# Attention and a gated feed-forward in one kernel: GpSimd's long instructions cut into pieces of 128 columns, and a pair of small VectorE instructions moved

## The chip, the cores and the metric

One Trainium2 chip; the kernel runs on one of its cores. The metric is the device time of a run in microseconds (us), lower is better. Engines: TensorE (PE, its weight loads PEld), VectorE (DVE), ScalarE (ACT), GpSimd (POOL), SyncE (SP), which issues most of the loads and stores.

## The reference

Attention over 4 batches, 8 heads, 576 tokens and 64 dimensions a head, with rotary positions on q and k, then a feed-forward of width 1024 with a convolution of three taps along the tokens and a gate:

```
q_rot, k_rot = rotate(q), rotate(k)      # [x1*cos - x2*sin, x1*sin + x2*cos]
scores = scale * q_rot @ k_rot^T
attn = exp(scores - max) / (sum + 1e-9)
x = (attn @ v) as [4, 576, 512]
h = max(x @ w_in, 0)
conv_out = conv_w[0]*h[s-1] + conv_w[1]*h[s] + conv_w[2]*h[s+1]
out = (h * sigmoid(conv_out)) @ w_out
```

The three weights reach the kernel as 64-bit floats; it converts them to 32 bits itself. q, k and v are 32-bit floats.

## The kernel before

The unit of attention is a pair of heads, p = 0 to 15. For each, q and k (512 of the tokens as [128, 4 x 2 x 64], "rq" and "rk"; the other 64 of both together, "rr") are loaded, rotated by `rope`, transposed on PE (`emit_TQ`), multiplied to scores (`emit_S`), reduced and turned into exponentials (`soft`: `negm` on DVE at L214, `st` on ACT at L218), transposed again (`emit_T`, `emit_Trem`), and multiplied with v (`emit_E`). For p=0 DVE does the rope of q and r, and POOL that of k; for all others POOL does all three. A rope is four instructions: two products with the tables of cosines and sines (L143 and L149, 512 columns for q or k, 128 for r), and two sums of half the columns (L155 and L156).

The sums of the exponentials come out of ACT's accumulator as `sums`, one column for each block of 128 queries. `emit_rinv` adds 1e-9 and takes the reciprocals on DVE, 9 columns each (L289, L290). `emit_rinvT` transposes these on PE (L295), copies them out ("rst"), and sends them through DRAM to come back spread over the partitions ("rb"), by which `norm` multiplies the product with v on DVE (L328).

The weights come in 16 pieces of 128 x 512. Each is converted by one ACT and four DVE instructions (`to_f32`: L446 to L460), then split into a high part, rounded by ACT (L503), and a low part, the difference, by POOL (L504). `conv_w` goes through the same code with 32 x 128 elements ("cwf"). The products of the feed-forward (`emit_M1` at L347, `emit_M2` at L425) use high and low parts. Between them DVE does the convolution (L359, L361) and the gate (L370), ACT the hyperbolic tangent, and ACT and POOL split the results ("g", at L378 and L379), as they split the attention's result ("xT", L332 and L333).

The order of the instructions is written out by hand: each engine runs its own in the order of emission. A plan holds entries (step, rank, function); five steps belong to a pair of heads. Within a step the ranks set the order, those of 10 and more come last, and after some entries a counter moves on, by which deferred work (`defer`) is emitted. Up to step 26 (`WIDE`) attention runs with the conversion of the weights; from there with the feed-forward's products, which are woven between the entries of rank 2 and 4; the last two blocks of the feed-forward run alone. The transposes of q, r and k of pair p stand at the steps 5p-4, 5p-3 and 5p-2 (`emit_TQ`), its ropes at 5p-8 and 5p-6. In the first stage ACT does the copies of `emit_Trem`, later DVE (L164). The instructions are placed like this:

```
at(max(n - 8, 0), 18, lambda p=p: rope(p, "q", nc.gpsimd))
at(max(n - 6, 0), 18, lambda p=p: rope(p, "k", nc.gpsimd))
at(n + 5, 4, lambda p=p: emit_E(p, 1))
at(n + 5, 1.7, lambda p=p: emit_rinv(p))
at(n + 6, 2, lambda p=p: emit_rinvT(p))
```

Of the kernel before, what the change touches and what calls it, by code (L numbers as in the profile page):

```python
# [7 lines left out]
F32 = mybir.dt.float32  # L8
# [4 lines left out]
ALU = mybir.AluOpType  # L13
# [7 lines left out]
def attention_moe_kernel(ctx, tc, q, k, v, w_in, conv_w, w_out, tab, out):  # L21
    nc = tc.nc
# [53 lines left out]
    def defer(k, fn, rank=1):  # L76
        due.setdefault(slot[0] + k, []).append((rank, len(due.get(slot[0] + k, [])), fn))
# [58 lines left out]
    def rope(p, part, eng):  # L136
        x = raw[p][part]
        n = 2 if part == "r" else 8
        if part != "r":
            x = x.rearrange("p t h d -> p (t h) d")  # L140
        c, s = (cosr, sinr) if part == "r" else (cosm, sinm)
        t1 = rot[p, part] = p1.tile([128, n, D], F32, tag="t1" + part, name="t1")
        eng.tensor_tensor(  # L143
            out=t1.rearrange("p n (e i) -> p n e i", e=2),
            in0=x.rearrange("p n (e i) -> p n e i", e=2),
            in1=c.unsqueeze(2).to_broadcast([128, n, 2, 32]),
            op=ALU.mult,
        )
        eng.tensor_tensor(  # L149
            out=x.rearrange("p n (e i) -> p n e i", e=2),  # L150
            in0=x.rearrange("p n (e i) -> p n e i", e=2),
            in1=s.unsqueeze(2).to_broadcast([128, n, 2, 32]),
            op=ALU.mult,
        )
        eng.tensor_tensor(out=t1[:, :, 0:32], in0=t1[:, :, 0:32], in1=x[:, :, 32:64], op=ALU.subtract)  # L155
        eng.tensor_tensor(out=t1[:, :, 32:64], in0=t1[:, :, 32:64], in1=x[:, :, 0:32], op=ALU.add)  # L156

    QT, KT = {}, {}

# [35 lines left out]
    def go(d, key):  # L195
        for fn in d.pop(key):
            fn()
# [58 lines left out]
    def emit_T(p, s, h=None):  # L256
        if p not in PT:
            PT[p] = ptp.tile([128, 9, S], F32, tag="pt", name="pt")
        pt = PT[p]
        ps = t_tile()  # L260
        st = STR[p] if s == 4 else ST[p, s][:, h, 64 * h:64 * h + 512]
        for t in range(4):
            nc.tensor.transpose(ps[:, 128 * t:128 * t + 128], st[:, 128 * t:128 * t + 128], idf)  # L263
        if s == 4:
            evac("A", pt[:, 0:8, 512:S], ps.rearrange("p (k c) -> p k c", k=8))
        else:
            evac("A", pt[:, h:8:2, 128 * s:128 * s + 128], ps.rearrange("p (k c) -> p k c", k=4))

    def emit_Trem(p, g):
        pt = PT[p]  # L270
        ps = t_tile()
        if g < 2:
            for u in range(2):
                x = ST[p, 2 * g + u].rearrange("p h k -> p (h k)")[:, 512:640]
                nc.tensor.transpose(ps[:, 128 * u:128 * u + 128], x, idf)
            evac("V", pt[:, 8, 256 * g:256 * g + 256], ps[:, 0:256])
        else:
            for h in range(2):
                x = strem[p % 2][:, 512 - 64 * h:640 - 64 * h]
                nc.tensor.transpose(ps[:, 128 * h:128 * h + 128], x, idf)  # L280
            for h in range(2):
                r = slice(64 * h, 64 * h + 64)
                evac("V", pt[r, 8, 512:S], ps[r, 192 * h:192 * h + 64])
# [3 lines left out]
    def emit_rinv(p):  # L287
        s = p % 2
        nc.vector.tensor_scalar(out=sums[p], in0=sums[p], scalar1=1e-9, scalar2=None, op0=ALU.add)  # L289
        nc.vector.reciprocal(out=rvc[s][:, 0:9], in_=sums[p])  # L290

    def emit_rinvT(p):
        s = p % 2
        ps = t_tile()[0:32, 0:128]
        nc.tensor.transpose(ps, rvc[s], idf)  # L295
        st = p1.tile([32, 128], F32, tag="rst", name="rst")
        evac("V", st, ps)
        d = scr.tile([9, 128], F32, tag="d", name="rd")
        nc.sync.dma_start(out=d, in_=st[0:9, :])
        fl = d.rearrange("(o t) n -> o (t n)", o=1)  # L300
        rbt = rb[p] = p1.tile([128, S], F32, tag="rb", name="rb")
        nc.sync.dma_start(out=rbt[0:64, :], in_=fl[:, 0:S].to_broadcast([64, S]))
        nc.sync.dma_start(out=rbt[64:128, 0:512], in_=fl[:, 640:1152].to_broadcast([64, 512]))
        nc.sync.dma_start(out=rbt[64:128, 512:S], in_=fl[:, 576:640].to_broadcast([64, 64]))
# [132 lines left out]
    def to_f32(pool, w64, w, n):  # L437
        w32 = w64.bitcast(I32).rearrange("p (n t) -> p n t", t=2)
        h, l = w32[:, :, 1], w32[:, :, 0]
        t = pool.tile([128, n], I32, tag="wt", name="wt")[0:w64.shape[0]]  # L440

        def first():
            nc.scalar.activation(out=t.bitcast(F32), in_=h.bitcast(F32), func=AF.Abs)  # L443

        def clamp():
            nc.vector.tensor_scalar(  # L446
                out=t.bitcast(F32), in0=t.bitcast(F32), scalar1=bits(F32_TINY), scalar2=bits(F32_HUGE),
                op0=ALU.max, op1=ALU.min,
            )

        def second():
            nc.vector.tensor_scalar(
                out=t, in0=t, scalar1=3, scalar2=0x3FFFFFFF, op0=ALU.logical_shift_left, op1=ALU.bitwise_and
            )
            nc.vector.scalar_tensor_tensor(
                out=t, in0=l, scalar=29, in1=t, op0=ALU.logical_shift_right, op1=ALU.bitwise_or
            )

        def third():
            nc.vector.scalar_tensor_tensor(  # L460
                out=w.bitcast(I32), in0=h, scalar=-(1 << 30), in1=t, op0=ALU.bitwise_and, op1=ALU.bitwise_or
            )

        return first, clamp, second, third
# [11 lines left out]
    def load_w(i):  # L476
        if i >= len(WPIECES):
            return
        src, _, _, kk, c = WPIECES[i]
        t = late["ws"].tile([128, 512], I64, tag="w64", name="w64", bufs=3)  # L480
        nc.sync.dma_start(out=t, in_=src[kk * 128:kk * 128 + 128, c:c + 512])
        stage[i] = t

    def conv_w_piece(i):
        _, dh, dl, kk, c = WPIECES[i]
        box = {}

        def first():
            box["w"] = late["ws"].tile([128, 512], F32, tag="wf", name="wf")
            box["s"] = to_f32(late["ws"], stage.pop(i), box["w"], 512)  # L490
            box["s"][0]()

        def mid():
            box["s"][1]()
            box["s"][2]()

        def third():
            box["s"][3]()
            load_w(i + 3)
            hi, lo = dh[:, kk, c:c + 512], dl[:, kk, c:c + 512]  # L500

            def split():
                nc.scalar.activation(out=hi, in_=box["w"], func=AF.Copy)  # L503
                nc.gpsimd.tensor_tensor(out=lo, in0=box["w"], in1=hi.bitcast(F32), op=ALU.subtract)  # L504

            defer(2, split)

        return [first, mid, third]
# [36 lines left out]
    def at(n, rank, fn):  # L545
        plan.setdefault(n, []).append((rank, len(plan.get(n, [])), fn))

    def emit():
        with tc.manual_schedule(engines=engines):
            load(0)  # L550
            for x in rvc + krem + [x[:, S:S + 64] for x in strem]:
                nc.vector.memset(x, 0.0)
            rope(0, "q", nc.vector)
            rope(0, "k", nc.gpsimd)
            rope(0, "r", nc.vector)
            for part in "qrk":
# [8 lines left out]
            for p in range(1, NP):  # L565
                n = STEPS * p
# [8 lines left out]
            for p in range(NP):  # L575
                n = STEPS * p
                for s in range(STEPS):
                    m = n + s
                    first = m < WIDE
                    if m:  # L580
                        at(m - 1 if first else m, 0.5 if first else 0, lambda p=p, s=s: emit_S(p, s))
                    at(m, 0.2, lambda p=p, s=s: go(reds, (p, s)))
                    at(m, 0.3 if first else 1.5, lambda p=p, s=s: go(exps, (p, s)))
                    for h in range(2 if s < 4 else 1):
                        at(m + 1, 0 if m + 1 < WIDE else 1, lambda p=p, s=s, h=h: emit_T(p, s, h))
                for g, e in ((0, 2), (1, 4), (2, 5)):
                    at(n + e, 2, lambda p=p, g=g: emit_Trem(p, g))
                at(n + 4, 4, lambda p=p: emit_E(p, 0))
                at(n + 5, 4, lambda p=p: emit_E(p, 1))
                at(n + 5, 1.7, lambda p=p: emit_rinv(p))  # L590
                at(n + 6, 2, lambda p=p: emit_rinvT(p))
                for j in range(2):
                    at(n + 8, 1.7 + j, lambda p=p, j=j: norms.pop((p, j))())
            nw = len(wsteps)
            for i, u in enumerate(wsteps):
                x = (WIDE - 1) * i // nw
# [114 lines left out]
```

## Time and profile before

| | |
|---|---|
| time, median of 3 runs | 556.59 us (555.76 to 556.72) |
| span of the profiled execution, first to last instruction | 553.1 us |
| PE busy | 508.9 us (92%) |
| DVE busy | 386.5 us (70%) |
| ACT busy | 325.1 us (59%) |
| POOL busy | 273.2 us (49%), 341 instructions |

The profile is of one execution, and its own time is known as its span; the median of the runs is 3.5 us above that. A busy share is an average over stages that differ. Matmuls are pipelined, and a busy PE may still wait between two of them. An instruction's duration includes the time in which it has started and can't go on.

### The profile page before, as it was taken

The page shows a single profiled execution, that of the slowest core. Times are in us where ns is not written, and L with a number is a line of the kernel's source. Part 1 is how long each engine was busy: PE and PEld are TensorE (multiplying, and loading weights), DVE is VectorE, ACT ScalarE, POOL GpSimd, SP SyncE. Part 2 cuts the span into 40 slices and gives each one's busy share as a digit, 9 for nine tenths or more (in the row PEclk, how much of TensorE's full clock was granted, in tenths as well). Part 3 has the DMA queues.
Part 4 walks back from the last instruction along what each step waited for, and adds up shares of the span by engine and source line. Part 5 has one row for each costly group of instructions (what it writes and reads, how often), then busy time and mean ns, then how long its engine had stood idle before and what let it go on. Part 6 is the DMA issues. An engine that isn't in the chain of part 4 may idle for free.

```text
span 553.1 us, 9298 instructions
## 1 busy us (share of the span) xinstructions
PE 508.9 (92%) x3295; PEld 369.3 (67%) x3295; DVE 386.5 (70%) x624; ACT 325.1 (59%) x870; POOL 273.2 (49%) x341
## 2 busy tenths in 40 slices
PE   2797969788999899999999999999999999999997
PEld 1354444445767477776877677777768677879986
DVE  4878977896588837684768747692677646657961
ACT  2779766877758545675747546663557546324530
POOL 4666857587573817383555637291361203232440
PEclk9999989999999999999999999999999999999999
DMA  7434433423303031030302140210300110000011
GB/s 187 130 101 130 121 104 97 142 75 71 87 1 87 1 83 24 24 84 7 99 2 66 40 106 1 62 45 26 101 0 24 41 42 0 29 33 20 2 38 58
DMA packets 67538, 33.08 MB, mean 60 GB/s; under 512 B 60412, under 2 KB 61220, under 8 KB 67492
## 3 DMA queue, kind: packets, MB, share of 16 engines
q1 hardware_dynamic: 66292, 32.10, 21.0%
q8 instruction: 26, 0.43, 0.3%
q10 hardware_dynamic: 1200, 0.39, 0.3%
q14 instruction: 20, 0.16, 0.1%
HBM read 27.68 MB, written 4.79 MB: 59 GB/s over the span
## 4 chain that ended last, share of the span: by engine, by line
PE 65%; DVE 15%; ACT 14%; issue 3%; DMA 2%; SPq 0%; ACTq 0%; DVEq 0%
PE tp L316 12%; PE sp L206 11%; PE pm L425 10%; PE pm L347 9%; PE tp L263 9%; PE mt L425 6%; ACT st L218 6%; PE mt L347 5%; DVE c L361 5%; ACT pt L162 4%; DVE negm L214 3%; DVE c L359 2%; PE tp L185 1%; DVE xn L328 1%; ACT wt L443 1%
## 5 line engine op out<-in xcount | busy, mean ns | idle before, releaser
L162 ACT ACTIVATE pt<-tp 128x512 f32<-128x512 f32 (+2 forms) x164 | 88.0, 562 | 93.1 <-PE tp L263 91.5
L214 DVE TENSOR_REDUCE negm<-sp 128x1 f32<-128x576 f32 x144 | 102.4, 748 | 39.5 <-PE sp L206 39.2
L379 POOL TENSOR_TENSOR g<-c,g 128x288 fp32r<-128x288 f32 (+4 forms) x88 | 57.0, 659 | 142.9 <-ACT g L378 141.3
L206 PE MATMUL sp<-kT,qT 64*128 64x288 f32 (+4 forms) x556 | 103.9, 470 | 1.2 <-ACT st L218 0.9
L218 ACT ACTIVATE st<-sp,negm 128x576 f32<-128x576 f32 x128 | 93.8, 746 | 15.1 <-DVE negm L214 15.1
L361 DVE SCALAR_TENSOR_TENSOR c<-rr,cw,c 128x288 f32<-128x288 f32 x128 | 96.7, 755 | 4.5
L263 PE MATMUL tp<-tabs,st 128*128 128x128 f32 x512 | 73.9, 285 | 20.3 <-ACT kr L162 7.6
L263 PEld LDWEIGHTS tp<-tabs,st 128*128 128x128 f32 x512 | 56.0, 143 | 46.2 <-issue 14.5
L347 PE MATMUL pm<-xT,winh 128*128 128x290 f32 x384 | 82.8, 308 | 0.5 <-ACT rr L355 0.5
L316 PE MATMUL tp<-pt,vm 128*64 128x290 f32 x512 | 69.6, 414 | 3.7 <-ACT pt L162 3.4
L206 PEld LDWEIGHTS sp<-kT,qT 64*128 64x128 f32 (+1 forms) x556 | 46.6, 177 | 36.0 <-issue 16.7
L425 PE MATMUL pm<-wouth,g 128*128 128x512 f32 x176 | 63.1, 412 | 0.0
L347 PEld LDWEIGHTS pm<-xT,winh 128*128 128x128 f32 x384 | 61.2, 190 | 1.4 <-ACT rr L355 0.7
L347 PE MATMUL pm<-xT,winl 128*128 128x290 f32 x192 | 56.9, 296 | 0.0
L370 DVE SCALAR_TENSOR_TENSOR c<-c,rr 128x288 f32<-128x288 f32 x64 | 39.1, 610 | 20.9 <-ACT c L367 20.2
L316 PEld LDWEIGHTS tp<-pt,vm 128*64 128x64 f32 x512 | 34.0, 136 | 28.8 <-ACT pt L162 5.1
L143 POOL TENSOR_TENSOR t<-rq,tabs 128x512 f32<-128x512 f32 x15 | 20.0, 1334 | 62.7 <-DMA rq<-q 62.1
L367 ACT ACTIVATE c<-c 128x288 f32<-128x288 f32 x64 | 28.3, 443 | 20.8 <-DVE c L361 20.5
L359 DVE TENSOR_SCALAR c<-rr,cw 128x288 f32<-128x288 f32 x64 | 31.2, 488 | 12.0 <-ACT rr L355 11.3
L425 PEld LDWEIGHTS pm<-wouth,g 128*128 128x128 f32 x176 | 33.1, 188 | 9.3 <-issue 2.2
L324 ACT ACTIVATE xn<-tp 128x290 f32<-128x290 f32 x32 | 13.2, 414 | 42.5 <-PE tp L316 42.5
L333 POOL TENSOR_TENSOR xT<-xn,xT 128x290 fp32r<-128x290 f32 x32 | 28.4, 892 | 18.2 <-ACT xT L332 16.9
(97 smaller groups left out, 883.6 us busy)
## 6 DMA issues: line engine op xcount, KB each, us to landing
out<-ot SPq DMA_DIRECT2D x17, 256.0 KB, 2.4
rk<-k SPq DMA_DIRECT2D x32, 128.0 KB, 3.0
w<-moe_w_in SPq DMA_DIRECT2D x8, 512.0 KB
vm<-v SPq DMA_DIRECT2D x32, 128.0 KB, 2.4
w<-moe_w_out SPq DMA_DIRECT2D x8, 512.0 KB, 3.4
rq<-q SPq DMA_DIRECT2D x30, 128.0 KB, 2.5
rb<-rd SPq DMA_DIRECT2D x16, 144.0 KB, 2.9
rb<-rd SPq DMA_DIRECT2D x16, 128.0 KB, 3.0
```

The costliest lines, as they stand in the source:

```text
L162: nc.scalar.activation(out=out, in_=in_, func=AF.Copy, scale=1.0 if sc is None else sc)
L206: nc.tensor.matmul(out=out, lhsT=qt[64 * h:64 * h + 64, c], rhs=kt[64 * h:64 * h + 64, a:a + n], start=True, stop=True)
L214: reds.setdefault((p, s), []).append(lambda: nc.vector.tensor_reduce(out=nm, in_=sc, axis=AX.XY if len(sc.shape) == 3 else AX.X, op=ALU.ma ...
L218: lambda: nc.scalar.activation(out=dst, in_=sc, func=AF.Exp, bias=nm, scale=1.0, accum_out=sm)
L263: nc.tensor.transpose(ps[:, 128 * t:128 * t + 128], st[:, 128 * t:128 * t + 128], idf)
L316: nc.tensor.matmul(out=xp[64 * h:64 * h + 64, 0:XW], lhsT=vmain[p][:, h, i, :] if i < 4 else vrem[p % 2][:, h, :], rhs=PT[p][:, 2 * i + h ...
L347: nc.tensor.matmul(out=ps[:, 0:XW], lhsT=w[:, kk, fs], rhs=xT[:, xs, e, :], start=(i == 0), stop=(i == n - 1))
L359: nc.vector.tensor_scalar(out=c, in0=r[:, j:j + HS], scalar1=cw[:, f:f + 1], scalar2=None, op0=ALU.mult)
L361: nc.vector.scalar_tensor_tensor(out=c, in0=r[:, j + e:j + e + HS], scalar=cw[:, 8 * e + f:8 * e + f + 1], in1=c, op0=ALU.mult, op1=ALU.add,)
L370: nc.vector.scalar_tensor_tensor(out=c, in0=c, scalar=1.0, in1=r[:, j + 1:j + 1 + HS], op0=ALU.add, op1=ALU.mult)
L379: nc.gpsimd.tensor_tensor(out=lo, in0=c[:, o:o + n], in1=hi.bitcast(F32), op=ALU.subtract)
L425: nc.tensor.matmul(out=ops[tt][:, 0:width], lhsT=g_tile(tt, f, e), rhs=w[:, f, cols], start=(f == 0 and i == 0), stop=(f == NF - 1 and i = ...
```

## The change

Two edits. In `rope`, where POOL does it, the two products go over two of the eight head blocks at a time (128 columns), and the two sums over four (128 columns of output); DVE's ropes stay whole. The low part of a piece of the weights is computed in four instructions of 128 columns. And `emit_rinv` moves from rank 1.7 to rank 4.5 of its step, behind the product with v of rank 4.

```diff
-        eng.tensor_tensor(
-            out=t1.rearrange("p n (e i) -> p n e i", e=2),
-            in0=x.rearrange("p n (e i) -> p n e i", e=2),
-            in1=c.unsqueeze(2).to_broadcast([128, n, 2, 32]),
-            op=ALU.mult,
-        )
...
-        eng.tensor_tensor(out=t1[:, :, 0:32], in0=t1[:, :, 0:32], in1=x[:, :, 32:64], op=ALU.subtract)
-        eng.tensor_tensor(out=t1[:, :, 32:64], in0=t1[:, :, 32:64], in1=x[:, :, 0:32], op=ALU.add)
+        t2, x2 = t1.rearrange("p n (e i) -> p n e i", e=2), x.rearrange("p n (e i) -> p n e i", e=2)
+        m = n if eng is nc.vector else 2
+        for dst, tb in ((t2, c), (x2, s)):
+            for a in range(0, n, m):
+                w = slice(a, a + m)
+                eng.tensor_tensor(
+                    out=dst[:, w], in0=x2[:, w], in1=tb[:, w].unsqueeze(2).to_broadcast([128, m, 2, 32]), op=ALU.mult
+                )
+        m = n if eng is nc.vector else min(n, 4)
+        for a in range(0, n, m):
+            w = slice(a, a + m)
+            eng.tensor_tensor(out=t1[:, w, 0:32], in0=t1[:, w, 0:32], in1=x[:, w, 32:64], op=ALU.subtract)
+            eng.tensor_tensor(out=t1[:, w, 32:64], in0=t1[:, w, 32:64], in1=x[:, w, 0:32], op=ALU.add)
...
-                nc.gpsimd.tensor_tensor(out=lo, in0=box["w"], in1=hi.bitcast(F32), op=ALU.subtract)
+                for o in range(0, 512, 128):
+                    w = slice(o, o + 128)
+                    nc.gpsimd.tensor_tensor(out=lo[:, w], in0=box["w"][:, w], in1=hi[:, w].bitcast(F32), op=ALU.subtract)
...
-                at(n + 5, 1.7, lambda p=p: emit_rinv(p))
+                at(n + 5, 4.5, lambda p=p: emit_rinv(p))
```

On POOL, at the start of the program, the rope of k of p=0 and the first instructions of that of q of p=1 stand like this before:

```order
L143 TENSOR_TENSOR t_118<-rk,tabs 128x512
L149 TENSOR_TENSOR rk<-rk,tabs 128x512
L155 TENSOR_TENSOR t_118<-t_118,rk 128x8x32
L156 TENSOR_TENSOR t_118<-t_118,rk 128x8x32
L512 MEMSET cw_177 32x256
L143 TENSOR_TENSOR t_195<-rq,tabs 128x512
```

And now, in the same place (the lines of the changed kernel have other numbers):

```order
L148 TENSOR_TENSOR t_118<-rk,tabs 128x128 x4
L148 TENSOR_TENSOR rk<-rk,tabs 128x128 x4
L154 TENSOR_TENSOR t_118<-t_118,rk 128x4x32
L155 TENSOR_TENSOR t_118<-t_118,rk 128x4x32
L154 TENSOR_TENSOR t_118<-t_118,rk 128x4x32
L155 TENSOR_TENSOR t_118<-t_118,rk 128x4x32
L514 MEMSET cw_185 32x256
L148 TENSOR_TENSOR t_203<-rq,tabs 128x128 x4
```

A rope of four instructions is now twelve; nothing else moved on POOL, and the order of its work is the same.

On DVE, in the step of the sums and reciprocals of p=5, the first pair of heads whose pair of instructions moved in the order, the queue is this before:

```order
L214 TENSOR_REDUCE negm<-sp 128x1 x2
L289 TENSOR_SCALAR sums<-sums 128x9
L290 RECIPROCAL rvc_83<-sums 128x9
L164 COPY pt<-tp 64x64 x2
L370 SCALAR_TENSOR_TENSOR c<-c,rr_1423 128x288
L359 TENSOR_SCALAR c<-rr_1424,cw 128x288
L361 SCALAR_TENSOR_TENSOR c<-rr_1424,cw,c 128x288 x2
L214 TENSOR_REDUCE negm<-sp 128x1 x2
```

And now:

```order
L213 TENSOR_REDUCE negm<-sp 128x1 x2
L163 COPY pt<-tp 64x64 x2
L369 SCALAR_TENSOR_TENSOR c<-c,rr_1575 128x288
L358 TENSOR_SCALAR c<-rr_1576,cw 128x288
L360 SCALAR_TENSOR_TENSOR c<-rr_1576,cw,c 128x288 x2
L288 TENSOR_SCALAR sums<-sums 128x9
L289 RECIPROCAL rvc_83<-sums 128x9
L213 TENSOR_REDUCE negm<-sp 128x1 x2
```

The pair went behind the copies, the gate of one part of the feed-forward and the convolution of the next. For p=5, 7, 9, 11, 13 and 15 it is so; for p=6, 8, 10, 12 and 14 the pair goes behind the two copies alone; for p=0 to 4 its place among DVE's instructions is the same. The queues of PE, ACT and SP are the same in both kernels.

## Rows read from the trace of the kernel before

**Rows 1.** The page's chain of waits that ended last, by engine.

```profile
PE 65%; DVE 15%; ACT 14%; issue 3%; DMA 2%; SPq 0%; ACTq 0%; DVEq 0%
```

**Rows 2.** Busy by stage: stretch, PE, PEld, DVE, ACT, POOL, granted clock, DMA share, GB/s.

```profile
14.00:146.00 132.00, 109.45 (x672) 62.14 (x669) 106.50 (x140) 100.50 (x260) 89.35 (x103) 0.96 0.37 104
146.00:411.00 265.00, 259.56 (x1758) 192.77 (x1757) 185.16 (x302) 159.36 (x433) 141.40 (x176) 1.00 0.19 48
```

**Rows 3.** Single lines on DVE: duration in ns, min/median/max, first and last start.

```profile
L361 DVE SCALAR_TENSOR_TENSOR c<-rr,cw,c x128: 517/522/1601, 147.7 to 531.5; 128x288 f32<-128x288 f32 x128
...
L214 DVE TENSOR_REDUCE negm<-sp x144: 694/748/760, 15.3 to 462.4; 128x1 f32<-128x576 f32 x144
...
L446 DVE TENSOR_SCALAR wt<-wt x17: 403/433/1387, 19.0 to 125.6; 128x512 f32<-128x512 f32 x16, 32x128 f32<-32x128 f32 x1
```

**Rows 4.** The same for lines of the rope on POOL.

```profile
L143 POOL TENSOR_TENSOR t<-rk,tabs x16: 1262/1366/1573, 6.6 to 405.5; 128x512 f32<-128x512 f32 x16
...
L143 POOL TENSOR_TENSOR t<-rr,tabs x15: 448/456/669, 15.7 to 403.7; 128x128 f32<-128x128 f32 x15
...
L155 POOL TENSOR_TENSOR t<-t,rk x16: 722/732/1054, 9.4 to 408.6; 128x256 f32<-128x256 f32 x16
```

**Rows 5.** Timeline of the start: start us, duration us, instruction.

```profile
6.64 1.26 POOL L143 TENSOR_TENSOR t<-rk,tabs 128x512 f32<-128x512 f32 x1 [6.20 <-DMA rk<-k]
6.67 1.51 DVE L156 TENSOR_TENSOR t<-t,rq 128x256 f32<-128x256 f32 x1
...
10.06 0.76 POOL L156 TENSOR_TENSOR t<-t,rk 128x256 f32<-128x256 f32 x1
...
11.37 1.06 PE L185 MATMUL tp<-tabs,t 128*128 128x128 f32 x4
```

**Rows 6.** Timeline: the end of the rope of q, p=1, and its transposes.

```profile
14.98 0.72 POOL L156 TENSOR_TENSOR t<-t,rq 128x256 f32<-128x256 f32 x1
...
20.29 0.66 PE L185 MATMUL tp<-tabs,t 128*128 128x128 f32 x4
```

**Rows 7.** Timeline of two places in the first stage; in brackets, idle time and releaser.

```profile
18.96 1.22 DVE L446 TENSOR_SCALAR wt<-wt 128x512 f32<-128x512 f32 x1
...
73.98 1.19 DVE L446 TENSOR_SCALAR wt<-wt 32x128 f32<-32x128 f32 x1 [3.48 <-ACT wt L443]
...
75.77 1.27 DVE L460 SCALAR_TENSOR_TENSOR cwf<-cw,wt 32x128 int32<-32x128 int32 x1
...
79.29 1.11 PE L263 MATMUL tp<-tabs,st 128*128 128x128 f32 x4 [3.62 <-ACT st L218]
```

**Rows 8.** Timeline around 105 us: two products on DVE, then ACT.

```profile
104.87 2.98 DVE L328 TENSOR_TENSOR xn<-xn,rb 128x290 f32<-128x290 f32 x2
...
108.55 0.74 ACT L218 ACTIVATE str<-sp,negm 128x576 f32<-128x576 f32 x1 [0.22 <-DVE negm L214]
```

**Rows 9.** A stretch of busy time (columns as in rows 2), and score matmuls.

```profile
80.00:82.00 2.00, 1.35 (x7) 0.95 (x7) 2.00 (x4) 1.82 (x4) 0.26 (x2) 0.50 0.00 0
...
82.53 2.08 PE L206 MATMUL sp<-kT,qT 64*128 64x512 f32 x4
...
89.05 1.13 PE L206 MATMUL sp<-kT,qT 64*128 64x512 f32 x4
```

**Rows 10.** Timeline around 190 us: DVE, and PE's wait for the copies.

```profile
187.30 1.38 DVE L359 TENSOR_SCALAR c<-rr,cw 128x288 f32<-128x288 f32 x1
...
191.79 0.16 DVE L289 TENSOR_SCALAR sums<-sums 128x9 f32<-128x9 f32 x1
...
192.11 0.40 DVE L164 COPY pt<-tp 64x64 f32<-64x64 f32 x2
...
192.56 0.71 PE L316 MATMUL tp<-pt,vr 128*64 128x290 f32 x4 [1.87 <-DVE pt L164]
```

**Rows 11.** Timeline: a convolution and the transpose of the reciprocals of p=5.

```profile
165.71 1.07 DVE L361 SCALAR_TENSOR_TENSOR c<-rr,cw,c 128x288 f32<-128x288 f32 x2
...
168.77 0.27 PE L295 MATMUL tp<-tabs,rvc 128*32 128x128 f32 x1
```

More of the change, by code (lines that the diff above doesn't have):

```diff
@@ L142, in rope @@
         t1 = rot[p, part] = p1.tile([128, n, D], F32, tag="t1" + part, name="t1")
-        eng.tensor_tensor(
-            out=t1.rearrange("p n (e i) -> p n e i", e=2),
-            in0=x.rearrange("p n (e i) -> p n e i", e=2),
-            in1=c.unsqueeze(2).to_broadcast([128, n, 2, 32]),
-            op=ALU.mult,
-        )
[L149 to L154, printed above, removed]
-        eng.tensor_tensor(out=t1[:, :, 0:32], in0=t1[:, :, 0:32], in1=x[:, :, 32:64], op=ALU.subtract)
-        eng.tensor_tensor(out=t1[:, :, 32:64], in0=t1[:, :, 32:64], in1=x[:, :, 0:32], op=ALU.add)
+        t2, x2 = t1.rearrange("p n (e i) -> p n e i", e=2), x.rearrange("p n (e i) -> p n e i", e=2)
[11 more added lines that the diff above has]
+            eng.tensor_tensor(out=t1[:, w, 32:64], in0=t1[:, w, 32:64], in1=x[:, w, 0:32], op=ALU.add)
     QT, KT = {}, {}
```

## The prediction

> **What bounds the kernel now.** I read the chain of waits first, for which engine the end hangs on, then the busy time by stage, then the shortest and longest time of single forms of instructions. The chain gives TensorE (PE) 65%, VectorE (DVE) 15% and ScalarE (ACT) 14% of the span [rows 1]. The stages differ. From 14 to 146 us, where attention runs with the conversion of the weights, PE has 109.45 us of 132 and is idle for 22.6; DVE has 106.50. From 146 to 411 us PE has 259.56 of 265 and is idle for 5.4 only [rows 2]. So the first stage can lose time where DVE is late, and the second has at most 5.4 us of idle PE to give. GpSimd (POOL) starts its last rope at 405.5 [rows 4], and the first one took 4.2 us [rows 5], so behind 411 us the pieces can change nothing.
>
> DVE's own durations show the wait that the change is about. The multiply-add of L361 takes 517 ns at best, 522 in the median and 1601 at worst for the same 288 columns, and L446 goes from 403 to 1387; the reduction of L214, which reads PSUM, stays between 694 and 760 [rows 3]. So some forms are stretched by up to 1.1 us and one is not. A place shows what stretches them: POOL starts a 512-column product at 6.64 and ends it at 7.90; DVE's L156, started at 6.67, lasts 1.51 us and ends at 8.18, just behind it [rows 5]. DVE waits for one POOL instruction, not for the four of the rope, and the last of the rope's, at 10.06 between DVE's, takes 0.76. I take from this that DVE gets through at every end of a POOL instruction, so the length of one POOL instruction bounds DVE's wait.
>
> The Trainium skill, page "SBUF — State Buffer", section "Who interferes with whom", says that the port pair between DVE and GpSimd is a lock that the first comer holds for its whole instruction, when the DVE instruction has two SBUF inputs or a two-port mode. The trace agrees for DVE. The same rule speaks against the change: a DVE instruction holds the pair against POOL too, and a rope in twelve pieces can be stopped twelve times; that is the second rival.
>
> **POOL's pieces.** A 512-column product takes 1262 ns at best, a 128-column one of the same line 448 (median 456) [rows 4]. Four pieces are 1.8 us, so each of the 62 products (31 ropes of q or k with two each) and each of the 16 low parts costs POOL 0.55 us more; a 256-column sum of 0.73 becomes two of about 0.46, so 0.19 more, 62 times. Together 78 x 0.55 + 62 x 0.19 = 55 us more for POOL, and a rope goes from 4.2 to about 5.5 us. What hides it: transposes come late. The narrowest case behind the first rope is q of p=1, whose last sum runs from 14.98 to 15.70 while PE's transposes start at 20.29: 4.6 us [rows 6]. The two ropes ahead add 1.3 each, 2.6 in all, so it still fits; without that cover the rest would be a PE wait. The loads into the raw tiles, which SP issues when the rope before has read them, move with the rope by the same 1.3 us and lie under the same cover.
>
> The first rope has no cover. POOL ends k of p=0 at 10.82 (10.06 + 0.76) and PE starts on it at 11.37 [rows 5], held until then by the r part on DVE. With pieces POOL ends near 6.64 + 5.5 = 12.1, with a little handed to DVE; PE starts at about 12.25. That is **+0.9 us** on the path (from +0.3 if pieces overlap at their ends, to +3.9 if each of the twelve takes the longest 128-column time, 669 ns, in place of the 4.2 us of now). DVE's r part is earlier, which nothing uses, since k is last.
>
> **DVE's waits.** A wait that found a 512-column instruction now finds a piece, of which half is left on average: 0.23 us (bounds 0 and 0.46). I price the places where the chain runs through a stretched DVE instruction.
> - At 18.96 L446 takes 1.22 in place of 0.40: wait 0.82, gain **0.6**.
> - At 73.98 and 75.77 the conversion of conv_w takes 1.19 and 1.27 [rows 7]. On 32 x 128 it can't need more than the 0.40 of the 512-column form, so the waits are at least 0.79 + 0.87; with two rests of 0.23 the gain is **1.2**. PE stands for 3.62 us until 79.29 behind it.
> - At 104.87 two products of L328 take 2.98 [rows 8]; by L361's shortest (nearly the same columns) 1.9 of it is wait. But ACT stood only 0.22 for the reduction behind them, so I take **0.8** between 0.2 and 1.9.
> - The clock. In the stretch from 80 to 82 us the granted clock is 0.50, the lower level of 1.2 GHz; PE did nothing from 76 until 79.29. The four score matmuls of 82.53 take 2.08, the same four at 89.05 take 1.13 [rows 9]: 0.95 lost there. If PE's idle time falls from 3.62 to about 2.4, the drop may come or not; other low matmuls count beside it. I take **0.9** of 0 to 1.9.
> - Of the remaining idle time of PE in this stage, some 18 us, I give a twelfth to the same waits elsewhere, **1.5** (0 to 4). This is the weakest term.
>
> From 146 to 411 us PE's idle time of 5.4 us is the ceiling. At 187.30 L359, with one tensor of 288 columns, takes 1.38, where L361 with two takes 0.52 at best; that lag reaches the copies of L164, for which PE stands 1.87 us at 192.56 [rows 10]. Shorter POOL instructions and the move below clear it. I take that and under half of the rest: **3.5** (1 to 5.4).
>
> **The move of the sums and reciprocals.** The order shows it at eleven of the sixteen pairs, from p=5 on. At five the pair goes behind the two copies of L164, at six behind a gate and a convolution as well. It took from 191.79 to 192.11, 0.32 us, ahead of the copies that PE waited for [rows 10]; where no PE wait stands on the copies it is worth nothing. This is inside the 3.5. The cost: the transpose of the reciprocals (L295) must not wait. For p=5 the second of the multiply-adds at 165.71 ends at 166.78 and L295 starts at 168.77 [rows 11]: 2.0 us for a pair of 0.4. Behind the pair DVE's queue has the two reductions of the next scores, which only change places with it. If this cover were gone, PE would wait, in order, for the pair. I price it at nothing.
>
> **The sum.** -0.6 - 1.2 - 0.8 - 0.9 - 1.5 + 0.9 - 3.5 = -7.6 us. The profiled execution has a span of 553.1; the median of the runs, 556.59, is 3.5 above it, which I take as outside the span and unchanged. So 545.5 for the span and **549.0 us** for the time.
>
> **Rivals.**
> 1. *The port time is only handed round.* There are 436 pieces in place of 140 instructions; at a wait of 0.23 for each, DVE would lose 100 us in all, more than it can. For it: DVE is busy for 106.50 of 132 us in the first stage, so the next instruction often stands ready when a piece starts. Against it: DVE's waits are single, with reductions in between that need no port. If each wait is a whole piece, 0.46, the first three gains fall to 0.4, 0.7 and 0.2, the clock and the other places to nothing, the second stage to 1, and the start costs 2: -0.3, so 556.3, no change. Chance 0.11.
> 2. *POOL becomes late, and the kernel slower.* Each piece is stopped by a DVE instruction. The place is the start: twelve pieces at 669 ns are 8.0 us, k of p=0 ends at 14.7 and everything moves by +3.9; q of p=1 keeps its distance, as PE is late too. For it: the skill's rule above, by which every piece may be stopped for a whole DVE instruction. Against it: the 128-column products exist already and their median, 456, is 8 ns over their best. It decides if the gains stay under 3.9, and can be measured if they stay under 2.8, a third of the 8.5 above; with a quarter, 2.1, the time is 556.6 + 3.9 - 2.1 = 558.4. Chance 0.10.
> 3. *All waits go.* The gains at their upper ends: 0.8 + 1.7 + 1.9 + 1.9 + 4 + 5.4 - 0.3 = 15.4, so 541.2. For it: few of the 128-column products of today stretch anything. Against it: the 288 and 290-column low parts of g and xT stay whole. Chance 0.15 for less than 544.
>
> **Chances and range.** The forecast's own range, 544 to 555, has 0.64. A change under 0.2%, 1.1 us, can't be told from none here. Faster 0.80 (the forecast, rival 3 and little else), the same 0.10, slower 0.10. The range from 541 to 557 leaves out the far side of rival 2 and gains beyond every upper bound.
>
> **What the profile after would show.** Right: L361 and L446 keep their shortest times and their worst fall to about 1 us or less, the remainder from 288-column POOL instructions; DVE's busy time falls by 25 us or more, POOL's rises by about 55; PE's first transposes of k at 12.2; the 3.62 at 79.29 under 2.5; no PE wait of over 0.5 us on L164's copies between 146 and 411; behind 411 us equal lengths. Wrong: if POOL's pieces are far above 0.46 or DVE's waits don't fall, the reading of the port is wrong; if DVE's time falls and the span doesn't, ACT or PE had been the bound in the first stage; if L295 waits, the move is.

## The result

The changed kernel takes 548.28 us (median of 4 runs, 547.00 to 548.66) against 556.17 (554.34 to 556.72) for the kernel before, a ratio of 0.9851 with a 95% interval of 0.9828 to 0.9875. A second measurement gave 549.16 against 556.68, 0.9861 [0.9826, 0.9895]. The span of the profiled execution is 546.8 us, 6.3 less than before. Everything read from a trace below compares two single executions, one of each kernel.

The page's chain of waits of the changed kernel, by engine, beside [rows 1]:

```profile
PE 80%; ACT 12%; DVE 3%; DMA 2%; issue 1%; POOL 1%; SPq 0%; ACTq 0%; POOLq 0%; DVEq 0%
```

DVE's share fell from 15% to 3%; POOL enters with 1%. Busy time by stretch, in the columns of [rows 2]: the two stages, then four stretches of 2 us.

```profile
14.00:146.00 132.00, 111.76 (x683) 63.91 (x680) 88.00 (x142) 101.42 (x266) 119.18 (x244) 0.96 0.38 107
146.00:411.00 265.00, 263.13 (x1797) 196.35 (x1794) 169.04 (x310) 159.43 (x433) 167.32 (x321) 1.00 0.19 47
...
28.00:30.00 2.00, 1.94 (x16) 1.14 (x12) 1.04 (x2) 2.00 (x6) 1.94 (x5) 1.00 0.64 166
76.00:78.00 2.00, 1.12 (x4) 0.72 (x4) 1.93 (x4) 2.00 (x6) 2.00 (x4) 0.65 0.77 254
80.00:82.00 2.00, 2.00 (x6) 0.50 (x5) 0.37 (x1) 1.82 (x5) 2.00 (x4) 0.50 0.36 70
86.00:88.00 2.00, 2.00 (x14) 1.06 (x11) 1.56 (x4) 0.24 (x1) 1.84 (x4) 0.79 0.00 0
```

From 146 to 411 us PE is idle for 1.87 us, where it was 5.44. From 14 to 146 DVE is busy for 18.5 us less, but PE gains only 2.3, and the granted clock is below full speed between 76 and 88 us, for some 10 us in all if it is counted as 0.50 (so again in the second profiled execution of this kernel); in the kernel before that was between 78 and 86, for some 7. An earlier low stretch of the kernel before, 26 to 32 us, some 3 of low clock, is gone. So the stage's mean granted clock is 0.96 in both; in these two executions the low clock only moved. Here is the middle of the earlier stretch and, after it, three PE instructions of the kernel before by which its lead can be read:

```profile
28.00:30.00 2.00, 2.00 (x9) 1.05 (x10) 0.32 (x1) 1.50 (x3) 1.27 (x1) 0.50 0.61 152
```

```profile
32.26 0.66 PE L263 MATMUL tp<-tabs,st 128*128 128x128 f32 x4 [0.37 <-ACT kT L162]
...
146.23 0.27 PE L175 MATMUL tp<-tabs,t 128*128 128x128 f32 x1
...
405.29 0.66 PE L316 MATMUL tp<-pt,vr 128*64 128x290 f32 x4
```

Single lines of the changed kernel on DVE and POOL, columns as in [rows 3] and [rows 4] (L360 and L445 were L361 and L446, L148 was L143 and L149):

```profile
L360 DVE SCALAR_TENSOR_TENSOR c<-rr,cw,c x128: 517/527/1166, 146.1 to 525.3; 128x288 f32<-128x288 f32 x128
...
L213 DVE TENSOR_REDUCE negm<-sp x144: 698/748/759, 15.4 to 456.0; 128x1 f32<-128x576 f32 x144
...
L445 DVE TENSOR_SCALAR wt<-wt x17: 378/494/699, 19.5 to 125.4; 128x512 f32<-128x512 f32 x16, 32x128 f32<-32x128 f32 x1
...
L148 POOL TENSOR_TENSOR t<-rk,tabs x64: 442/454/737, 6.6 to 400.7; 128x128 f32<-128x128 f32 x64
```

The shortest times of L360 and L445 stand nearly where they were, the longest fell by 0.44 and 0.69 us, and the reduction from PSUM did not change. The median of L445 rose from 433 to 494: more of them wait a little, and none waits long. POOL's piece keeps to 454 ns in the median, 12 over its best; some are stretched, in this line to 737. The timeline of the changed kernel at the places of [rows 5] to [rows 11]:

```profile
6.56 2.01 POOL L148 TENSOR_TENSOR t<-rk,tabs 128x128 f32<-128x128 f32 x4 [6.12 <-DMA rk<-k]
6.66 0.67 DVE L155 TENSOR_TENSOR t<-t,rq 128x256 f32<-128x256 f32 x1
...
11.10 1.51 PE L184 MATMUL tp<-tabs,t 128*128 128x128 f32 x4 [1.50 <-POOL t L155]
11.42 0.45 POOL L155 TENSOR_TENSOR t<-t,rk 128x128 f32<-128x128 f32 x1
...
16.60 0.44 POOL L155 TENSOR_TENSOR t<-t,rq 128x128 f32<-128x128 f32 x1
...
19.49 0.70 DVE L445 TENSOR_SCALAR wt<-wt 128x512 f32<-128x512 f32 x1
...
20.59 0.66 PE L184 MATMUL tp<-tabs,t 128*128 128x128 f32 x4
...
31.02 0.66 PE L262 MATMUL tp<-tabs,st 128*128 128x128 f32 x4 [1.08 <-ACT kT L161]
...
72.71 0.38 DVE L445 TENSOR_SCALAR wt<-wt 32x128 f32<-32x128 f32 x1 [4.73 <-ACT wt L442]
...
74.02 0.43 DVE L459 SCALAR_TENSOR_TENSOR cwf<-cw,wt 32x128 int32<-32x128 int32 x1
...
76.70 1.12 PE L262 MATMUL tp<-tabs,st 128*128 128x128 f32 x4 [2.29 <-ACT st L217]
...
83.15 3.98 PE L315 MATMUL tp<-pt,vm 128*64 128x290 f32 x16 [0.28 <-DVE cw L527]
...
88.36 1.13 PE L205 MATMUL sp<-kT,qT 64*128 64x512 f32 x4
...
103.36 1.34 DVE L327 TENSOR_TENSOR xn<-xn,rb 128x290 f32<-128x290 f32 x2
...
144.60 0.27 PE L174 MATMUL tp<-tabs,t 128*128 128x128 f32 x1
...
163.97 0.22 DVE L289 RECIPROCAL rvc<-sums 128x9 f32<-128x9 f32 x1
...
166.49 0.27 PE L294 MATMUL tp<-tabs,rvc 128*32 128x128 f32 x1
...
187.59 0.66 PE L315 MATMUL tp<-pt,vr 128*64 128x290 f32 x4
...
398.97 0.66 PE L315 MATMUL tp<-pt,vr 128*64 128x290 f32 x4
```

The queue of PE is the same in both kernels, so the same instruction in both timelines gives PE's lead. It is 1.24 us at 32.26 (now 31.02), 2.59 at 79.29 of [rows 7] (now 76.70), 0.69 at 89.05 of [rows 9] (now 88.36), 1.63 at 146.23 (now 144.60), 4.97 at 192.56 of [rows 10] (now 187.59), 6.32 at 405.29 (now 398.97), and 6.3 at the end. Two things are to be read off. Between 79 and 89 us 1.90 us are given back, in the low clock, in which sixteen products with v take 3.98 us. And the second stage, from 146 to 405 us, is worth 4.7.

### The profile page after: what moved, and what is told of

It reads as the page before. It is cut to its first block, busy times and chain, and to the rows that moved or that the text cites. A ratio compares the mean times of both kernels' runs of the same rounds, so it can differ in the third digit from the quotient of the medians.

```text
span 546.8 us, 9601 instructions
## 1 busy us (share of the span) xinstructions
PE 508.6 (93%) x3295; PEld 370.0 (68%) x3295; DVE 345.7 (63%) x624; ACT 322.6 (59%) x870; POOL 329.2 (60%) x637
## 4 chain that ended last, share of the span: by engine, by line
PE 80%; ACT 12%; DVE 3%; DMA 2%; issue 1%; POOL 1%; SPq 0%; ACTq 0%; POOLq 0%; DVEq 0%
PE tp L315 16%; PE sp L205 14%; PE pm L346 13%; PE tp L262 11%; PE pm L424 11%; PE mt L424 6%; PE mt L346 5%; ACT st L217 5%; ACT pt L161 4%; PE tp L184 2%; PE tp L274 1%; ACT wt L442 1%; DVE c L360 1%; DMA rk<-k 1%; ACT kT L161 1%
## 5 line engine op out<-in xcount | busy, mean ns | idle before, releaser
L378 POOL TENSOR_TENSOR g<-c,g 128x288 fp32r<-128x288 f32 (+4 forms) x88 | 55.8, 645 | 123.6 <-ACT g L377 123.6
L360 DVE SCALAR_TENSOR_TENSOR c<-rr,cw,c 128x288 f32<-128x288 f32 x128 | 80.7, 631 | 4.5
L315 PE MATMUL tp<-pt,vm 128*64 128x290 f32 x512 | 71.4, 422 | 3.7 <-ACT pt L161 3.4
L148 POOL TENSOR_TENSOR t<-rq,tabs 128x128 f32<-128x128 f32 x60 | 30.6, 539 | 49.7 <-DMA rq<-q 45.3
L369 DVE SCALAR_TENSOR_TENSOR c<-c,rr 128x288 f32<-128x288 f32 x64 | 38.4, 600 | 18.5 <-ACT c L366 17.9
L346 PEld LDWEIGHTS pm<-xT,winl 128*128 128x128 f32 x192 | 36.7, 191 | 0.0
L358 DVE TENSOR_SCALAR c<-rr,cw 128x288 f32<-128x288 f32 x64 | 27.4, 429 | 11.7 <-ACT rr L354 11.0
```

The lines of the kernel that those rows point to most:

```text
L148: eng.tensor_tensor(out=dst[:, w], in0=x2[:, w], in1=tb[:, w].unsqueeze(2).to_broadcast([128, m, 2, 32]), op=ALU.mult)
L315: nc.tensor.matmul(out=xp[64 * h:64 * h + 64, 0:XW], lhsT=vmain[p][:, h, i, :] if i < 4 else vrem[p % 2][:, h, :], rhs=PT[p][:, 2 * i + h ...
L346: nc.tensor.matmul(out=ps[:, 0:XW], lhsT=w[:, kk, fs], rhs=xT[:, xs, e, :], start=(i == 0), stop=(i == n - 1))
L360: nc.vector.scalar_tensor_tensor(out=c, in0=r[:, j + e:j + e + HS], scalar=cw[:, 8 * e + f:8 * e + f + 1], in1=c, op0=ALU.mult, op1=ALU.add,)
L369: nc.vector.scalar_tensor_tensor(out=c, in0=c, scalar=1.0, in1=r[:, j + 1:j + 1 + HS], op0=ALU.add, op1=ALU.mult)
L378: nc.gpsimd.tensor_tensor(out=lo, in0=c[:, o:o + n], in1=hi.bitcast(F32), op=ALU.subtract)
```

## The experiments

**Each edit by itself.** First the changed kernel with the low parts of the weights whole again and the sums and reciprocals back at their place; only the ropes are cut.

```diff
-                for o in range(0, 512, 128):
-                    w = slice(o, o + 128)
+                for o in range(0, 512, 512):
+                    w = slice(o, o + 512)
...
-                at(n + 5, 4.5, lambda p=p: emit_rinv(p))
+                at(n + 5, 1.7, lambda p=p: emit_rinv(p))
```

> Only the ropes are cut into 128 columns; low parts of the weights whole, sums and reciprocals at their old place. Port theory (VectorE waits for the one GpSimd instruction that runs, so its length sets the wait): most of the gain is the ropes', since they alone run behind 146 us: 549.5 to 551.5 us, the multiply-add of the convolution near 640 ns in the mean (755 before), the copies of VectorE before the product with v waited for under 0.6 us. Rival (the move of the sums and reciprocals clears the wait of 1.87 us and the pieces matter little): 555 to 556. Rival (the low parts of the weights, in the first stage, are the main wait): 553 to 555.

Then only the weights' low parts are cut (the ropes' m is n or min(n, 8), the pair stands at 1.7).

```diff
-        m = n if eng is nc.vector else 2
+        m = n if eng is nc.vector else min(n, 8)
...
-        m = n if eng is nc.vector else min(n, 4)
+        m = n if eng is nc.vector else min(n, 8)
...
-                at(n + 5, 4.5, lambda p=p: emit_rinv(p))
+                at(n + 5, 1.7, lambda p=p: emit_rinv(p))
```

> Only the low parts of the weights are cut. Port theory: nothing changes behind 146 us, and in the first stage the conversions on VectorE wait less behind GpSimd's low parts: 555 to 556 us, 0.5 to 1.5 us less than before. If the low parts are the main wait: 551 to 553. If the pieces cost GpSimd more than they give: 556.5 to 557.5.

And the kernel before with the pair moved, and nothing else.

```diff
-                at(n + 5, 1.7, lambda p=p: emit_rinv(p))
+                at(n + 5, 4.5, lambda p=p: emit_rinv(p))
```

> Only the sums and reciprocals are moved; all GpSimd instructions as before. Port theory: the pair of 0.3 to 0.8 us no longer stands ahead of the copies that TensorE waits for, at three or four places: 555 to 556 us, about 1 us less. Rival (the move is the cause of the gain): 549 to 552. If the transposes of the reciprocals now wait: 557 or more.

Measured, against 556.17 of the kernel before on the same chip: ropes alone 549.12, 0.9873 [0.9843, 0.9903]; weights alone 553.75, 0.9955 [0.9924, 0.9985]; the move alone 553.75, 0.9962 [0.9937, 0.9986]. The ropes alone gave a little more than I had expected, and the other two lie 1.3 us below the lower end of it. The three gains add up to 11.9 us, where together they gave 7.9: what the smaller two give alone is not added to what the ropes give. The second stage of the three, in this order, in the columns of [rows 2]:

```profile
146.00:411.00 265.00, 263.12 (x1796) 196.21 (x1795) 169.36 (x310) 159.50 (x436) 167.52 (x321) 1.00 0.19 48
```

```profile
146.00:411.00 265.00, 258.89 (x1758) 192.07 (x1758) 185.92 (x304) 158.86 (x427) 141.34 (x176) 1.00 0.18 47
```

```profile
146.00:411.00 265.00, 259.67 (x1759) 192.81 (x1758) 184.23 (x300) 159.32 (x432) 141.29 (x176) 1.00 0.19 48
```

The ropes alone give PE the 263.1 us of the whole change there, the other two leave it at the 259 to 260 of before. PE's lead, read at the same two instructions as above (146.23 and 405.29 in the kernel before), grows by 4.67 between them with the ropes alone, by nothing with the move alone (-0.22 and -0.21), and shrinks by 0.63 with the weights alone. So in these executions the whole gain of the second stage is that of the ropes, and none of it the move's. The weights, converted up to about 140 us, can act in the first stage only. Their effect is seen at two places. One is conv_w, in the second kernel's PE timeline, where the sixteen products run at full clock, as in the kernel before (with the ropes alone PE stands 2.85 us there):

```profile
78.23 0.66 PE L262 MATMUL tp<-tabs,st 128*128 128x128 f32 x4 [2.29 <-ACT st L217]
...
84.23 2.17 PE L315 MATMUL tp<-pt,vm 128*64 128x290 f32 x16 [0.28 <-DVE cw L527]
```

The other is L327 near 104 us: its two products take 1.34 us with the weights alone, with the ropes alone, and with both, and PE's wait of 0.62 us at 115.95 in the kernel before, for a copy of ACT's, is gone in all three.

What the move alone gave in the medians is not in its profiled execution (553.3 us of span against 553.1). It isn't the clock alone: at a mean granted clock of 0.991 three of its runs took 551.3 to 553.7 us, and five of the kernel before on that chip 554.5 to 556.8. Where it comes from stays open; the experiment at the end of this section asks what is left of it once the pieces are short.

**Longer and shorter pieces.** The changed kernel with pieces of 256 and of 64 columns, in the ropes' products and sums and in the weights (for 64 in place of 128: m is min(n, 1) and min(n, 2), and the range below goes in steps of 64).

```diff
-        m = n if eng is nc.vector else 2
+        m = n if eng is nc.vector else min(n, 4)
...
-        m = n if eng is nc.vector else min(n, 4)
+        m = n if eng is nc.vector else min(n, 8)
...
-                for o in range(0, 512, 128):
-                    w = slice(o, o + 128)
+                for o in range(0, 512, 256):
+                    w = slice(o, o + 256)
```

> The changed kernel with pieces of 256 columns (products of the rope, low parts of the weights; sums of the rope whole, they have 256 columns already). Port theory: VectorE's longest wait is between that of 512 and of 128 columns, 0.7 us, so the multiply-add's mean lies between 631 and 755 ns, near 680, and the time between: 549.5 to 552 us. If only the number of GpSimd's instructions or the moved pair counted: 548 or 555.

> Pieces of 64 columns everywhere (those of the 64 remaining tokens too). Port theory: VectorE waits less again, 0.3 us at most behind a piece, but the 288-column low parts of g and xT stay, and GpSimd has some 400 instructions more of 0.32 us: its busy time goes from 329 to some 370 to 390 us, the first rope ends 1.5 to 2.5 us later, and the time is 548.5 to 551, no better. Rival (the shorter the better): 545.5 to 547.5. Rival (GpSimd becomes late, transposes wait for the rope): above 552.

The changed kernel itself ran once more beside the second of them:

> The changed kernel as it is, beside the next three on the same chip, to compare them with. 547 to 549.5 us.

256 columns: 549.23, 0.9880 [0.9850, 0.9910], which can't be told from 128 here. 64 columns: 578.81 against 556.68, 1.0401 [1.0366, 1.0435]; slower by 22 us than the kernel before. The changed kernel: 549.16. What the piece's length does to DVE shows in the mean of the multiply-add on the profile's page: 755 ns before, 678 with 256 columns and 631 with 128, at an unchanged best of 517 (busy us and mean ns behind the bar, then idle time before):

```profile
L361 DVE SCALAR_TENSOR_TENSOR c<-rr,cw,c 128x288 f32<-128x288 f32 x128 | 96.7, 755 | 4.5
```

```profile
L360 DVE SCALAR_TENSOR_TENSOR c<-rr,cw,c 128x288 f32<-128x288 f32 x128 | 86.8, 678 | 4.5
```

```profile
L360 DVE SCALAR_TENSOR_TENSOR c<-rr,cw,c 128x288 f32<-128x288 f32 x128 | 80.7, 631 | 4.5
```

With 64 it is 629, no longer less. Of 64 columns, first the durations of the conversion's first instruction on DVE and of POOL's pieces; then PE's waits for ACT's exponentials and for POOL (us in total, times, longest); then the timeline around the longest L445, with all POOL rows behind its start:

```profile
L445 DVE TENSOR_SCALAR wt<-wt x17: 405/595/5026, 20.6 to 144.3; 128x512 f32<-128x512 f32 x16, 32x128 f32<-32x128 f32 x1
...
L148 POOL TENSOR_TENSOR t<-rk,tabs x128: 310/318/772, 5.9 to 432.4; 128x64 f32<-128x64 f32 x128
```

```profile
PE sp L205 <- ACT st L217: 7.5, 4, 5.6
...
PE tp L184 <- POOL t L155: 6.2, 9, 2.5
```

```profile
125.40 5.03 DVE L445 TENSOR_SCALAR wt<-wt 128x512 f32<-128x512 f32 x1
125.45 0.32 POOL L155 TENSOR_TENSOR t<-t,rq 128x64 f32<-128x64 f32 x1
125.73 0.32 POOL L154 TENSOR_TENSOR t<-t,rq 128x64 f32<-128x64 f32 x1
126.01 0.32 POOL L155 TENSOR_TENSOR t<-t,rq 128x64 f32<-128x64 f32 x1
126.29 2.26 POOL L505 TENSOR_TENSOR woutl<-wf,wouth 128x64 fp32r<-128x64 f32 x8
128.51 1.55 POOL L332 TENSOR_TENSOR xT<-xn,xT 128x290 fp32r<-128x290 f32 x2
130.02 1.04 POOL L148 TENSOR_TENSOR t<-rr,tabs 128x64 f32<-128x64 f32 x2
```

Two things happen. A piece of 64 columns costs 318 ns, 70% of one of 128, so POOL is busy for 404 us and late: PE stands for it nine times, for 6.2 us. That is what the second rival said would come of it, but not by its mechanism: the median piece is 8 ns over its best, so what makes POOL late is the price of a piece and not that DVE stops each. And DVE does not get through at every end of a POOL instruction: L445, 0.41 us of work, ran from 125.40 to 130.43 while POOL began instruction behind instruction, the short ones 0.28 apart. Eight DVE instructions took over 3 us in this run; in the changed kernel none took over 1.17. PE's longest single wait behind the start, 5.6 us at 174.73, is for exponentials that came late behind another of them (3.49 us at 168.55). The clock adds its part: the mean granted clock is 0.973 and not 0.991, and PE's busy time is 521.3 us and not 508.6. What makes DVE fail between short pieces and succeed between those of 128 isn't settled: in both, the next piece starts about 0.04 us before the last one ends.

**The low parts that stayed whole.** The changed kernel with the low parts of g and xT (288 and 290 columns) in halves too.

```diff
-            nc.gpsimd.tensor_tensor(out=xT[:, sl, 1, :], in0=xn, in1=xT[:, sl, 0, :].bitcast(F32), op=ALU.subtract)
+            for u in range(0, XW, 145):
+                w = slice(u, u + 145)
+                nc.gpsimd.tensor_tensor(
+                    out=xT[:, sl, 1, w], in0=xn[:, w], in1=xT[:, sl, 0, w].bitcast(F32), op=ALU.subtract
+                )
...
-                nc.gpsimd.tensor_tensor(out=lo, in0=c[:, o:o + n], in1=hi.bitcast(F32), op=ALU.subtract)
+                for u in range(0, n, 144):
+                    w = slice(u, min(u + 144, n))
...
```

> The changed kernel, and the low parts of g (288 columns) and xT (290) in two pieces of 144 and 145 as well. Port theory: VectorE's worst wait falls from 0.65 to about 0.35 us, its busy time by 8 to 12 us; TensorE has little idle time left behind 146 us, so the time changes by -0.3 to -1.5: 546.5 to 548. If the pieces make the last block's low parts late: 548.5 to 550.

548.07, 0.9850 [0.9816, 0.9884], beside 549.16 for the changed kernel, whose runs cover the same range: no difference that shows. The longest multiply-add falls from 1169 to 850 ns, so what was left of its wait was behind these low parts. DVE's busy time falls by another 7 us, from 344.4 to 337.6, and PE doesn't notice: from 146 to 411 us it had only 1.87 us of idle time left.

**The conversion of conv_w moved.** In the changed kernel the five small DVE instructions of conv_w stand at step 12, rank 3, ahead of two reductions of scores; PE's stand of 2.29 us and the low clock follow them. Here they stand behind these.

```diff
-            at(12, 3, conv_cw)
+            at(13, 0.25, conv_cw)
```

> The changed kernel with the conversion of conv_w behind the reductions of step 13, in place of ahead of them. In the profile after, TensorE stands 2.29 us at 76.7 us behind it, the granted clock is low from 77 to 87.6 us and the lead over the kernel before falls from 2.59 to 0.69 us. If that stall is what lowers the clock there: no low clock between 74 and 90 us and 3 to 5 us less, 543.5 to 545.5. If the clock falls for another reason (what TensorE did in the whole stage): 1 to 2 us less, 546 to 547.5. If ScalarE's turn decides, not VectorE's queue: no change.

543.62 (543.40 to 545.08), 0.9773 [0.9737, 0.9809]: 5.5 us below the changed kernel beside it. Its PE timeline at the place, and the lowest of the stretches around it:

```profile
76.71 0.84 PE L262 MATMUL tp<-tabs,st 128*128 128x128 f32 x4 [1.57 <-ACT kT L161]
...
81.05 2.17 PE L315 MATMUL tp<-pt,vm 128*64 128x290 f32 x16 [0.28 <-DVE cw L527]
```

```profile
78.00:80.00 2.00, 2.00 (x5) 0.50 (x6) 1.80 (x3) 1.97 (x6) 2.00 (x4) 0.50 0.01 2
```

The wait for the softmax is gone; one of 1.57 for a copy of ACT's is left. The sixteen products with v take 2.17 us, where the changed kernel's took 3.98. Counted as above, the clock is low for 3.4 us between 76 and 82 (0.76, 0.50 and 0.89 in the three stretches) in place of 10. I had expected none; in the three other profiled executions with cut pieces and conv_w later, below, it is 1.00 from 74 to 90 us. Four of the other five runs of this kernel had a mean granted clock of 0.999 or 1.000.

**What is left of the edits without the low clock.** The same move in the kernel before, in the kernel with 256 columns, and in the changed kernel with the pair of sums and reciprocals at its old place; and once more the changed kernel with it alone.

```diff
-            at(12, 3, conv_cw)
+            at(13, 0.25, conv_cw)
...
-                at(n + 5, 4.5, lambda p=p: emit_rinv(p))
+                at(n + 5, 1.7, lambda p=p: emit_rinv(p))
```

The second edit is that of the third kernel alone.

> The kernel before with one number changed: conv_w's rounding runs at step 13 and 0.25 and not at step 12 and 3, on the queue of deferred work; GpSimd's instructions stay whole. Theory A (two separate costs: the stand at 76 to 79 us with the low clock behind it belongs to the place of conv_w, the rest to GpSimd's instruction length): 3.6 us of PE standing on the softmax and about half of the 5 us of extra time in low clock behind it go, 551 to 553.5 us against 556.5. Theory B (the gain of the move comes only together with cut pieces, because whole pieces lock VectorE out wherever the chain stands): 555 to 557 us, with a PE wait of over 2 us on the softmax elsewhere between 74 and 84 us.

> The changed kernel with rope and the low parts of the weights in pieces of 256 columns and not 128, and with conv_w's rounding at step 13 and 0.25. Theory A (256 and 128 columns are worth the same, since no VectorE instruction on the chain is late by more than PE's slack at either length): 543 to 544.5 us, as the 128-column kernel with conv_w later. Theory B (128 columns matter once the low-clock stretches are gone): 1 us or more above it.

> The changed kernel with conv_w's rounding at step 13 and 0.25, and with the sums and reciprocals at their old place (1.7). Tells what their move is worth where little low clock blurs it. Theory A (the move is worth the DVE waits behind the four places from 146 to 411 us, about 0.5 us each): 545 to 546 us against 543.6 with the move. Theory B (once GpSimd's pieces are short the copies behind the sums come in time from either place): the same within 0.4 us.

> The changed kernel with conv_w's rounding at step 13 and 0.25, once more, as the reference of the three beside it: 543.4 to 545 us, no low clock before 74 us, at most some 5 us of it behind.

| | median, us | runs | ratio to before (555.02) |
|---|---|---|---|
| before, conv_w later | 552.73 | 549.63 to 556.64 | 0.9965 [0.9936, 0.9995] |
| 256 columns, conv_w later | 545.98 | 544.98 to 547.35 | 0.9842 [0.9802, 0.9881] |
| 128 columns, conv_w later, pair at 1.7 | 543.88 | 543.17 to 545.45 | 0.9805 [0.9769, 0.9841] |
| 128 columns, conv_w later | 543.56 | 543.38 to 544.84 | 0.9801 [0.9766, 0.9837] |

The place of the pair is worth nothing with cut pieces (543.88 and 543.56). Six runs of 256 columns all lie above the six of 128, by 2.4 us in the median: the shorter piece does matter, once the low clock no longer covers it. And the later conv_w gives the kernel before 2.3 us, in the range of theory A, but its profile speaks partly for B: whole POOL instructions hold DVE at the new place too. That profile is of the longest of its twelve runs (556.64 us), so it shows what can happen there, and not what the median owes to it. Its timeline:

```profile
77.06 1.64 DVE L455 SCALAR_TENSOR_TENSOR wt<-w,wt 128x512 int32<-128x512 int32 x1
78.62 1.87 DVE L328 TENSOR_TENSOR xn<-xn,rb 128x290 f32<-128x290 f32 x2
...
80.62 0.24 PE L524 MATMUL tp<-tabs,cwf 32*128 32x32 f32 x1 [1.66 <-ACT pt L162]
81.92 4.13 PE L316 MATMUL tp<-pt,vm 128*64 128x290 f32 x16 [1.06 <-DVE cw L525]
```

PE stands for 1.66 us on a copy of ACT's and for 1.06 on DVE's copy of conv_w, and the products with v run at the low clock again (4.13 us).

## Why the prediction was right

**The span, and what lies around it.** I forecast 545.5 us for the span; it is 546.8. The 3.5 us that I put outside the span are 1.8 in every run here (548.66 - 546.8, 549.11 - 547.3); by that I estimate 554.9 us for the profiled execution of the kernel before, less than each of its three runs. So the terms gave 6.3 of the 7.6 us forecast, and 1.7 us too many outside the span hid that. That 549.0 and 548.28 lie so close is luck.

**DVE waits for one POOL instruction.** Right for the change: L155 beside the first piece takes 0.67 us and not 1.51, DVE's busy time fell by 41 us (386.5 to 345.7) and POOL's rose by 56 (273.2 to 329.2), where I had worked out 55. The worst of L360 is 1166 ns, a little over the 1 us that I gave, at 476.90 beside a 290-column low part of xT; another of 1165, at 511.46, starts beside a 288-column one of g. Both kinds stay whole, and cut in halves they leave 850. But the sentence that DVE gets through at every end of a POOL instruction is wrong as a rule: it holds at 128, 256 and 512 columns, and 64 columns break it (5.03 us).

The Trainium skill, page "SBUF — State Buffer", section "Who interferes with whom", has the pair held by one instruction at a time. The runs agree down to 128 columns, where no multiply-add waited over 0.65 us (1166 - 517 ns); at 64 a wait of some 4.6 us over fifteen POOL instructions goes beyond it.

**The start, +0.9.** Mis-sized: about +0.2. PE's transposes of k ran from 11.37 to 12.43 [rows 5] and now run from 11.10 to 12.61. I had let PE wait for the last piece, at 12.1; it is done at 11.87, and PE takes the two first blocks when the first pair of sums is ready. The last sum of q of p=1 ends at 17.04, PE comes at 20.59: the cover held.

**conv_w, -1.2.** Right in mechanism and size: 0.38 and 0.43 us in place of 1.19 and 1.27, and PE's stand is 2.29 and not 3.62. Its lead rose from 1.24 to 2.59 up to there. The weights' pieces alone bring the same stand of 2.29.

**The clock, -0.9.** This step failed, by its sign. A shorter stand did not bring a shorter low stretch: the lead falls from 2.59 to 0.69, a loss of 1.90. I took only the lower bound, zero, as the bad case. The stretch from 26 to 32 us, which I had not looked at, was low before and is not now, and it makes up what I called "other places" (-1.5): the lead goes from -0.3 at 20.29 [rows 6] to 1.24 at 32.26. That the size agrees is luck. I had put it on idle time, and the waits there gave about nothing; eight transposes and eight score products at full clock took 1.56 us less. Nor do short pieces rule that stretch out: with 128 columns it is there in the profiled execution with the low parts in halves (clock 0.70 and 0.50 from 26 to 30 us) and in the one with conv_w later and the pair at 1.7 (0.72 and 0.50). The 18.96 term (0.6) failed as a term of its own: L445 takes 0.70, 0.52 less, and no PE instruction waits on it by itself.

**L328, -0.8.** Right in size: the pair takes 1.34 us in place of 2.98, and between 89 and 146 us the lead grows by 0.94. Nearly all of it comes at 115.95, where PE's wait of 0.62 us for ACT is gone; ACT had stood 1.25 us at 113.45 for a reduction of DVE's, which was late.

**The first stage together** is therefore -1.6 and not -4.1 (shorter waits, less the start, gave some 2.0, the moved low clock took some 0.3), **the second** -4.7 and not -3.5. Of the latter, 3.3 come up to the place that I named, where PE stood for 1.87 at 192.56 and now, at 187.59, doesn't. That it was the ropes, and that the move of the pair adds nothing to them, the experiments say and I did not: I had put the move inside the term. Its cost, zero, was right: the reciprocals of p=5 end at 164.19 and PE transposes them at 166.49.

**Behind 411 us** nothing changed, as said: the lead is 6.32 at 405.29 and 6.3 at the end.

**The rivals.** The first (port time handed round) is out: DVE's busy time fell by 41 us. The outcome of the second, POOL late, came at 64 columns, by the price of a piece. The time of the third, below 544, needed one more edit, the later conv_w, and came by PE's shorter stand and the clock there.

## What to carry to other kernels

Cut an instruction of the engine that shares a port only as far as the other engine's wait stops falling: here 512 to 256 gave most, 128 another 2.4 us once nothing else covered it, and 64 made the kernel 22 us slower than with whole instructions, since a piece has a price of its own and DVE no longer always came between. Price a low-clock stretch as a risk of both signs: when a stand is shortened but stays, look whether the work that causes it can be moved instead, which was worth 5.5 us here for one number. And where a change has several edits, run each alone early: the ropes alone gave 7.1 of the 7.9 us of this one.

## What the runs showed of the hardware that was not expected

- DVE can be kept waiting through a row of short GpSimd instructions: 5.03 us over fifteen of them, mostly of 64 columns, while beside 128-column pieces no DVE instruction took over 1.17 us. Why is open.
- PE stood for 2.29 us in the changed kernel, and the clock was at its lower level, 1.2 GHz, for some 10 us behind it; with only the weights cut, the same 2.29 us at the same place were followed by some 3.4 us (0.64 and 0.51 in the two stretches from 80 to 84), and in the kernel before 3.62 us by some 7. The stand alone doesn't set the length.
- Runs of one kernel spread with their mean granted clock, though not by it alone: of its eleven runs beside the second measurement, the kernel before took 556.8 to 559.3 us in the five at 0.985 and 553.2 to 556.7 in the six at 0.988 to 0.997; with conv_w later, where the mean was 0.996 to 1.000, six runs lay within 1.7 us.
